# Fewer warm-up products, and four of the first pair's maxima between its first score groups

## The chip, the cores and the metric

One core of a Trainium2 chip runs the whole program. The metric is the time of one execution in microseconds on the device, as a median of runs; smaller is better. The engines are named as in the profile: PE is TensorE (matrix products), PEld its weight load, DVE VectorE, ACT ScalarE, POOL GpSimd, and SP issues the DMA transfers.

## The reference

Three stages, one after the other, all in fp32:

```
q_pool = q.reshape(B, H, S // 2, 2, D).mean(axis=3)
scores = scale * np.matmul(q_pool, k.transpose(0, 1, 3, 2))
scores = scores - np.max(scores, axis=-1, keepdims=True)
attn = np.exp(scores)
attn = attn / (np.sum(attn, axis=-1, keepdims=True) + 1e-09)
x = np.matmul(attn, v)                    # B 4, H 8, S 1152, D 64
h = x @ w_in                              # 2304 tokens, 512 to 2048
g = np.where(h > 0.0, h, np.exp(np.minimum(h, 0.0)) - 1.0)
y = g @ w_out                             # 2048 to 512
...                                       # soft mixture of 8 experts over y
```

## The kernel before

**Attention.** The 32 heads are taken in 16 pairs. For a pair, q is loaded and neighbours summed (`pool_q`, line 556), q and k are transposed by PE against an identity and split into a high and a low part (`prep_q`, lines 574 to 583; `prep_k`, lines 597 to 605, in two pieces of six and three blocks). The score groups (line 682, 36 for a pair) hold keys on the partitions, so the maximum over keys has to be known before the exponential. It is found ahead, from products of the high parts alone: a maximum unit (line 613, `max_unit`) makes 128 query rows (64 in the last tile) times 384 keys for both heads in PSUM, and DVE reduces it (line 622, `max_red`). The first pair has 15 such units of its own: nine for the first half of its queries and six for the second, of these six three with 128 rows and three with 64. When a half is complete, `max_end` reduces once more (DVE, line 662), lays the result out as a row with three products (PE, line 658), and ACT writes its negative (line 666); a score group of that half adds this row as its last two products. The exponential is ACT's (line 694), the running sum of exponentials POOL's or DVE's (line 703), and the product with v is line 689. For the later pairs most maxima ride along inside the score groups of the pair before.

**PSUM.** Score groups, maximum units and transposes share three double banks (psA0, psA1, psS2), taken in turn. A unit holds its bank until DVE has reduced it, a score group until ACT has taken its exponential.

**Warm-up.** The first work of PE is a row of 100 products of a constant with itself (`warm`, line 723), into psC1; nothing reads them. psC1 is then used by the second piece of k.

**Order.** Every operation has a planned time. A planner sorts them by these times and by a cost model of its own, and writes out one fixed order for each engine; on the chip each engine works its list in that order and waits for what an entry needs. The times of the first pair's six units for its second half stand in the table `MAX1`, as distances in groups of two score steps and an offset; those of `max_end` stand in `DE`.

**After attention** come an ELU network in 32 slots (lines 850 and 889) and the soft mixture of experts, whose weights are loaded into buffers as these come free (line 1214).

Of the kernel before, what the change touches and what calls it, by code (L numbers as in the profile page):

```python
# [26 lines left out]
def act(n, psum=False):  # L27
    return n * 0.0009 + (0.135 if psum else 0.165)
# [22 lines left out]
class Plan:  # L51
# [11 lines left out]
    def add(self, t, eng, dur, fn, r=(), w=(), size=0.0, mode="F", port=False, fixed=False):  # L63
        if isinstance(eng, str):
            eng, dur = (eng,), (dur,)
        cls = (self.tag or str(self.phase)) + "".join(x.rstrip("0123456789") for x in w[0][:2] if isinstance(x, str)) + (eng[0] if len(eng) == 1 else "*")
        self.ops.append([t, len(self.ops), eng, dur, fn, r, w, size * (0.75 if self.phase == 2 else 1.0), BIAS[3 if self.tag else self.phase], t + PRI.get(cls, 0.0), cls, mode, port, fixed])
# [194 lines left out]
N3 = 10  # L262
TM2 = [-14.582, 27.792, 22.6349, 17.3721]
TDT = [0.625, 1.728, 6.6355, 1.2]
WARM = [100]
OFF = {'wi': -10.8492, 'wo': 0.9719, 'h': -0.5713, 'o': -0.4908}
EP = 1.3
SLOT = 14.8061
# [2 lines left out]
DQ = [-10, 0.61]  # L271
DK = [[-9, 0.3], [-9, 0.3]]
UC = -14
MAX1 = [[-4, 0.9], [-3, 0.9], [-3, 1.3], [-2, 0.4], [0, 0.9], [0, 1.3]]
MAX2 = [[[-7, 0.4], [-6, -0.1], [-5, -0.1], [-4, -0.1]], [[-2, -0.1], [-1, -0.1]]]
DE = [[-2, 0.3], [2, 0.5]]
SUMD = [[1, 0.1], [1, 0.3]]
# [8 lines left out]
def attention_moe_softmoe(  # L286
# [99 lines left out]
    def v3(ap, a):  # L386
        return ap.rearrange("p (a b) -> p a b", a=a)
# [152 lines left out]
    def load_q(p, t):  # L540
        b, h0 = heads(p)
        for j in range(2):
            dma(t, QR[:QP, j].rearrange("p c r d -> p c (r d)"), q[b, h0 + j].rearrange("(c p r) d -> p c (r d)", p=QP, r=2),
                [], [("QR", 0, j)], 295e3)

    def load_k(p, t):
        b, h0 = heads(p)
        for j in range(2):
            dma(t, KR[:, :, j], k[b, h0 + j].rearrange("(p c) d -> p c d", c=NC), [], [("KR", 0, j)], 295e3)

    def load_v(p, t):
        b, h0 = heads(p)
        dma(t, VR[p % 2], v[b, h0 : h0 + 2].rearrange("h (p c) d -> p h c d", c=NC), [], [("VR", p % 2)], 590e3, 0.45)

    def pool_q(p, t):
        add(t, ("DVE", "Pool") if p else ("DVE",), (dve(768), pool(768))[: 1 + (p > 0)], lambda e="DVE": ENG[e].tensor_tensor(  # L556
            NQt[:QP].rearrange("p c j d -> p j c d"), QR[:QP, :, :, 0, :], QR[:QP, :, :, 1, :], ALU.add),
            r=[("QR", 0, 0), ("QR", 0, 1)], w=[("NQ", 0)], port=True)

    def T(p, d, x):  # L560
        return (NU * p + 2 * d) * STEP + x

    def TG(p, d, x):
        return (NU * p + GU * d) * STEP + x

    TC = 0.5 * GU * STEP

    def prep_q(p, t):
        i = p % 2
        tok = ("S", "pq", p)  # L570

        def tr():
            for c in range(QC):
                nc.tensor.transpose(got(psS, tok)[:, c // 3, c % 3 * QP : (c % 3 + 1) * QP],  # L574
                                    NQt[:QP, c].rearrange("p j d -> p (j d)"), ident[:QP, :QP])

        def ps():
            return got(psS, tok)[:, :, :NH]

        hi, lo = v3(qkb["qh", i], 2), v3(qkb["ql", i], 2)  # L580
        add(t, "PE", QC * 0.109, tr, r=[("NQ", 0)], w=[tok, ("qh", i), ("ql", i)], fixed=True)
        add(t + 0.01, "ACT", act(NQ, True), lambda: nc.scalar.copy(hi, ps()), r=[tok], w=[("qh", i)])
        add(t + 0.02, "DVE", dve(NQ), lambda: nc.vector.tensor_tensor(lo, ps(), r32(hi), ALU.subtract), r=[tok, ("qh", i)], w=[("ql", i)])

    def prep_k(p, g, t):
        i = p % 2
        lo_c, hi_c = KG[g]
        m = hi_c - lo_c
        nb = m // 3
        tok = ("S", "pk", p, g) if nb == 2 else ("C", 1)  # L590

        def bk(x):
            return got(psS, tok)[:, x] if nb == 2 else psC[1]

        def tr():
            for x in range(m):
                nc.tensor.transpose(bk(x // 3)[:, x % 3 * P : (x % 3 + 1) * P], KR[:, lo_c + x].rearrange("p j d -> p (j d)"), ident)  # L597

        def ps():
            return got(psS, tok)[:, :, : 3 * P] if nb == 2 else v3(psC[1][:, : 3 * P], 1)  # L600

        hi, lo = (v3(qkb[n, i][:, lo_c * P : hi_c * P], nb) for n in ("kh", "kl"))
        add(t, "PE", m * 0.109, tr, r=[("KR", 0, 0), ("KR", 0, 1)], w=[tok, ("kh", i, g), ("kl", i, g)], fixed=True)
        add(t + 0.01, "ACT", act(m * P, True), lambda: nc.scalar.copy(hi, ps()), r=[tok], w=[("kh", i, g)])
        add(t + 0.02, "DVE", dve(m * P), lambda: nc.vector.tensor_tensor(lo, ps(), r32(hi), ALU.subtract),
            r=[tok, ("kh", i, g)], w=[("kl", i, g)])
# [21 lines left out]
    def max_unit(p, a, g, t):  # L628
        tok = ("S", "max", p, a, g)
        add(t, "PE", 0.172, lambda: max_mm(got(psS, tok), p, a, g, 2, 0), r=max_deps(p, g, 2), w=[tok], mode="R", fixed=True)  # L630
        max_red(tok, p, a, g, 2, 0, t + 0.01)

    carry, own = {}, {}
    for p in range(NP):
        own[p] = []
        cells = {h: [(a, g) for a in ((0, 1, 2), (3, 4))[h] for g in range(0, NM, 2)] for h in range(2)}
        if p == 0:
            own[p] = [(a, g, *((-7 + x // 2, 0.2 * (x % 2)) if GU == 2 else (-5 + x // 3, 0.2 * (x % 3)))) for x, (a, g) in enumerate(cells[0])]
            own[p] += [(a, g, *MAX1[x]) for x, (a, g) in enumerate(cells[1])]
            continue  # L640
# [9 lines left out]
    def max_end(p, h, t):  # L650
        i = p % 2
        tiles = (0, 1, 2) if h == 0 else (2, 3, 4)

        def row():
            for a in tiles:
                o, n = QT[a]
                lo, hi = max(o, h * NH), min(o + n, (h + 1) * NH)
                nc.tensor.matmul(psC[h][:D, lo - h * NH : hi - h * NH], lhsT=MZ[:, a].rearrange("p j m -> p (j m)"), rhs=IDR[:, lo - o : hi - o],
                                 start=True, stop=True)

        a0, a1 = tiles[0] if h == 0 else 3, tiles[-1] + 1
        add(t - 0.5, "DVE", 0.2, lambda: nc.vector.reduce_max(MZ[:, a0:a1, :, 0], MX[i][:, a0:a1], axis=AX.X),
            r=[("MX", i, a, g) for a in range(a0, a1) for g in range(NM) if (p, a, g) in cells_of], w=[("MZ", 0, a) for a in range(a0, a1)])
        add(t, "PE", 0.15, row, r=[("MZ", 0, a) for a in tiles], w=[("C", h)], mode="C", fixed=True)
        for j in range(2):
            add(t + 0.01 + 0.01 * j, "ACT", act(NH, True), lambda j=j: nc.scalar.mul(
                v3(qkb["nm", i], 2)[j * D : j * D + D // 2, h], psC[h][j * D // 2 : (j + 1) * D // 2, :NH], -1.0), r=[("C", h)], w=[("nm", i, h, j)])
# [59 lines left out]
    def warm_first(n):  # L727
        f = MEM["v"][:, ND - 256 :]
        add(-101, "DVE", 0.5, lambda: None, w=[("vone", 0)])
        warm(n, -99.9, f, [("vone", 0)])  # L730
# [17 lines left out]
    for p in range(NP):  # L748
        if p == 0:
            plan.tag = "P"  # L750
            warm_first(WARM[0])
        load_q(p, T(p, -19.5, 0))
        load_k(p, T(p, -16.5, 0))
        load_v(p, T(p, -6, 0))
        pool_q(p, T(p, -11, 0))
        prep_q(p, TG(p, DQ[0], TC + DQ[1]))
        for g in range(2):
            prep_k(p, g, TG(p, DK[g][0] if p else (-9 if GU == 2 else -6), TC + DK[g][1] + 0.01 * g))
        for a, g, d, y in own[p]:
            max_unit(p, a, g, TG(p, d, y))  # L760
        for h in range(2):
            max_end(p, h, TG(p, DE[h][0], TC + DE[h][1]))
        plan.tag = None
        for u in range(NU):
            step(p, u)
# [608 lines left out]
```

## Time and profile before

| | |
|---|---|
| median of three runs | 1008.2 us (1007.24 to 1009.51) |
| the profiled execution | 1009.69 us, with a span of 1007.9 us |
| mean granted clock of PE | 0.981 |
| PE busy | 968.3 us, 96% |
| DVE busy | 763.3 us, 76% |
| ACT busy | 497.0 us, 49% |
| POOL busy | 396.8 us, 39% |

The profile is of one execution. Starts are in microseconds from the start of its span; a granted clock of 1.00 is full speed (2.4 GHz) and 0.50 is half (1.2 GHz). Matrix products are pipelined, so one that is shown as 280 ns long can be followed by the next after 118 ns; the distance of two starts says what one costs.

### The profile page before, as it was taken

Reading aid. Unit: us, or ns where it says so; the run is one execution under the profiler, and the core shown is the slowest. Engines: PE = TensorE matmul, PEld = TensorE weight load, DVE = VectorE, ACT = ScalarE, POOL = GpSimd, SP = SyncE. Lnnn points to the kernel's source line nnn. Section 1 sums busy time; section 2 is a strip of 40 time slices with the busy share of each in tenths; the row PEclk is TensorE's granted clock in tenths of the full one; section 3 lists DMA queues with packets and bytes.
Section 4 is the critical chain, followed back from the end, with each engine's and each line's share of the span. In section 5 each row is a group of like instructions: output and inputs, shape, how many; then the busy total and the mean of one; then the engine's idle time right before and its main releaser. Section 6 shows DMA issues by size and latency. Waiting matters only on the chain.

```text
span 1007.9 us, 21047 instructions
## 1 busy us (share of the span) xinstructions
PE 968.3 (96%) x8550; PEld 791.4 (79%) x8550; DVE 763.3 (76%) x1281; ACT 497.0 (49%) x887; POOL 396.8 (39%) x278
## 2 busy tenths in 40 slices
PE   7999999999999999999999999999999999998965
PEld 5677777766777767666899999999999999996422
DVE  4777788888878788899998899889857887765103
ACT  1466565565666656565664444434434475443102
POOL 1588879878888878887300000000000000000000
PEclk9799999999999999999999999999999999998997
DMA  7233323325334323221263233324430132315798
GB/s 170 47 78 79 82 64 103 90 61 157 97 84 103 84 67 82 62 68 34 78 224 106 99 114 107 116 84 152 152 123 26 42 123 88 119 49 230 258 379 281
DMA packets 101584, 114.88 MB, mean 114 GB/s; under 512 B 43632, under 2 KB 70768, under 8 KB 101488
## 3 DMA queue, kind: packets, MB, share of 16 engines
q1 hardware_dynamic: 101488, 113.55, 36.9%
q8 instruction: 67, 1.10, 0.4%
q14 instruction: 29, 0.24, 0.1%
HBM read 100.27 MB, written 13.18 MB: 113 GB/s over the span
## 4 chain that ended last, share of the span: by engine, by line
PE 83%; DVE 9%; DMA 5%; issue 1%; ACT 1%; SPq 1%; DVEq 0%; POOL 0%; ACTq 0%; POOLq 0%
PE psC L889 20%; PE psA L850 20%; PE psC L689 13%; PE psA L682 10%; PE psS L682 4%; DMA memf<-in_moe_w_dram 3%; PE psA L613 3%; DVE memf L622 2%; PE psS L613 2%; PE psC L723 1%; PE psC L713 1%; PE psA L597 1%; DMA memzq<-in_moe_w_dram 1%; DVE memf L556 1%; PE psA L574 1%
## 5 line engine op out<-in xcount | busy, mean ns | idle before, releaser
L703 POOL TENSOR_TENSOR memf<-memf 128x576 f32<-128x576 f32 x241 | 360.2, 1497 | 62.7 <-ACT memf L694 38.3
L889 PE MATMUL psC<-memr,memz 128*128 128x288 f32 x1512 | 224.7, 297 | 1.2 <-DVE memf L900 0.7
L889 PEld LDWEIGHTS psC<-memr,memz 128*128 128x128 f32 x1512 | 208.1, 188 | 4.4 <-ACT memf L508 1.6
L689 PE MATMUL psC<-memf 128*64 128x288 f32 x1152 | 174.2, 419 | 0.0
L694 ACT ACTIVATE memf<-psA 128x576 f32<-128x576 f32 x207 | 133.5, 652 | 63.7 <-PE psA L613 51.1
L622 DVE TENSOR_REDUCE memf<-psA 128x2 f32<-128x384 f32 (+3 forms) x236 | 143.3, 619 | 27.2 <-PE psA L613 13.0
L1334 POOL MEMSET memf<- 128x2048 f32 x1 | 1.8, 1811 | 388.5 <-DVE memr L511 388.5
L900 DVE TENSOR_TENSOR memf<-psC,memf 128x288 f32<-128x288 f32 x220 | 100.3, 463 | 47.9 <-PE psC L889 46.2
L622 DVE TENSOR_REDUCE memf<-psS 128x2 f32<-128x384 f32 (+1 forms) x139 | 102.6, 738 | 35.3 <-PE psS L613 18.7
L689 PEld LDWEIGHTS psC<-memf 128*64 128x64 f32 x1152 | 69.8, 136 | 48.5 <-issue 9.2
L850 PE MATMUL psA<-memz 128*128 128x288 f32 x512 | 93.8, 295 | 0.0
L861 ACT ACTIVATE memf<-psA 128x576 f32<-128x576 f32 x64 | 41.8, 654 | 103.1 <-PE psA L850 103.0
L508 ACT CAST memr<-memf 128x576 fp32r<-128x576 f32 x72 | 48.2, 675 | 74.3 <-PE psC L889 35.9
L850 PEld LDWEIGHTS psA<-memz 128*128 128x128 f32 x512 | 76.6, 188 | 0.0
L682 PE MATMUL psA<-memr 64*128 64x288 f32 x816 | 72.2, 299 | 2.9 <-DVE memf L622 2.9
L694 ACT ACTIVATE memf<-psS 128x576 f32<-128x576 f32 x81 | 52.8, 652 | 39.3 <-PE psS L613 35.9
L511 DVE TENSOR_TENSOR memr<-memf,memr 128x576 fp32r<-128x576 f32 x80 | 62.8, 791 | 6.5 <-ACT memr L508 6.0
L682 PEld LDWEIGHTS psA<-memr 64*128 64x128 f32 x816 | 59.2, 185 | 9.7 <-DVE memf L622 4.8
L682 PE MATMUL psA<-memy 64*128 64x288 f32 x630 | 62.6, 304 | 0.1
L850 PE MATMUL psA<-memz,memv 128*128 128x288 f32 x256 | 52.0, 296 | 0.0
L682 PEld LDWEIGHTS psA<-memy 64*128 64x128 f32 x630 | 47.8, 188 | 4.9 <-issue 3.6
L508 ACT COPY memf<-psC 128x288 f32<-128x288 f32 (+1 forms) x66 | 26.3, 398 | 49.5 <-PE psC L1265 26.6
(213 smaller groups left out, 1623.2 us busy)
## 6 DMA issues: line engine op xcount, KB each, us to landing
memf<-wscr SPq DMA_DIRECT2D x32, 512.0 KB
memf<-in_moe_w_dram SPq DMA_DIRECT2D x30, 512.0 KB
memzq<-in_moe_w_dram SPq DMA_DIRECT2D x22, 512.0 KB
memz<-in_q_dram SPq DMA_DIRECT2D x32, 288.0 KB
memz<-in_k_dram SPq DMA_DIRECT2D x32, 288.0 KB
memf<-in_v_dram SPq DMA_DIRECT2D x16, 576.0 KB
memf<-in_moe_w_in_dram SPq DMA_DIRECT2D x32, 256.0 KB
wscr<-memf SPq DMA_DIRECT2D x32, 256.0 KB
```

The costliest lines, as they stand in the source:

```text
L508: return lambda e: nc.scalar.copy(out_, in_) if e == "ACT" else nc.vector.tensor_copy(out_, in_)
L511: return lambda e: ENG[e].tensor_tensor(out_, a, b, ALU.subtract)
L613: nc.tensor.matmul(tile_[:m, j, lo : lo + n * MW], lhsT=qkb["qh", i][js, o : o + m], rhs=qkb["kh", i][js, g * MW : (g + n) * MW], start=Tr ...
L622: add(t, "DVE", dve(2 * n * MW), lambda: nc.vector.reduce_max(MX[i][:m, a, :, g : g + n], v4(got(psS, tok)[:m, :, lo : lo + n * MW], n), a ...
L682: nc.tensor.matmul(sp[:, j, :NH], lhsT=qkb[w, i][js, cs] if w else ONER[js], rhs=qkb[m, i][js, hs], start=(x == 0), stop=(x == 3))
L689: nc.tensor.matmul(psC[h][j * D : (j + 1) * D, :NH], lhsT=VR[i][:, j, c], rhs=e[:, j], start=(c == 0), stop=(c == NC - 1))
L694: add(t + 0.01, "ACT", act(NQ, True), lambda: nc.scalar.activation(got(EAf, E_), got(psS, S_)[:, :, :NH], AF.Exp, scale=1.0 / 16.0), r=[S_ ...
L703: ENG[e].tensor_tensor(ac, a, got(EAf, E_), ALU.add)
L850: nc.tensor.matmul(ph[:, t, :NH], lhsT=a, rhs=x, start=(i == 0), stop=(i == 3 * KD - 1))
L861: add(t, "ACT", act(NQ, True), lambda: nc.scalar.activation(got(Ef, uk), ph(), AF.Relu, scale=-1.0), r=[A], w=[uk])
L889: nc.tensor.matmul(po_(), lhsT=a, rhs=x, start=(i == 0), stop=(i == 3 * GF - 1))
L900: add(t0 + 0.8, "DVE", dve(NH), lambda: nc.vector.tensor_tensor(d, po_(), d, ALU.add), r=[ck], w=XK)
```

## The change

The warm-up has 24 products in place of 100. The table `MAX1` gives the six units of the second half other times, all later, and the first pair's `max_end` gets a table `DE1` of its own, whose times are 0.3 and 0.1 us later than in `DE`.

```
-WARM = [100]
+WARM = [24]
...
-MAX1 = [[-4, 0.9], [-3, 0.9], [-3, 1.3], [-2, 0.4], [0, 0.9], [0, 1.3]]
+MAX1 = [[-2, 0.4], [-2, 1.3], [0, -0.1], [0, 0.9], [1, -0.1], [1, 1.3]]
+DE1 = [[-2, 0.6], [2, 0.6]]
...
-            max_end(p, h, TG(p, DE[h][0], TC + DE[h][1]))
+            max_end(p, h, TG(p, (DE if p else DE1)[h][0], TC + (DE if p else DE1)[h][1]))
```

The lines of the changed kernel below the tables are one higher than before. On PE, the piece from the eleventh unit to just ahead of the third score group stands so before (`ident` with `memf` is the transpose of the second pair's q, `ident` with `memz0` that of its k, line 682 a score group in two rows):

```order
L613 MATMUL psA0_78<-memy_95 128x384 x2
L613 MATMUL psA1_79<-memy_95 128x384 x2
L613 MATMUL psS2_85<-memy_95 64x384 x2
L658 MATMUL psC0_80<-memv_94 64x128 x2
L658 MATMUL psC0_80<-memv_94 64x32
L574 MATMUL psA0_78<-ident_65,memf_93 128x96 x6
L682 MATMUL psA1_79<-memy_95 128x288 x6
...
L613 MATMUL psA1_79<-memy_95 64x384 x2
L613 MATMUL psA0_78<-memy_95 64x384 x2
L597 MATMUL psS2_85<-ident_65,memz0_96 128x128 x6
L597 MATMUL psC1_81<-ident_65,memz0_96 128x128 x3
```

And so in the changed kernel, up to the first product with v:

```order
L614 MATMUL psA0_78<-memy_95 128x384 x2
L659 MATMUL psC0_80<-memv_94 64x128 x2
L659 MATMUL psC0_80<-memv_94 64x32
L575 MATMUL psA1_79<-ident_65,memf_93 128x96 x6
L614 MATMUL psS2_85<-memy_95 128x384 x2
L683 MATMUL psA0_78<-memy_95 128x288 x6
...
L614 MATMUL psA0_78<-memy_95 64x384 x2
L598 MATMUL psA1_79<-ident_65,memz0_96 128x128 x6
L598 MATMUL psC1_81<-ident_65,memz0_96 128x128 x3
L614 MATMUL psS2_85<-memy_95 64x384 x2
...
L614 MATMUL psA0_78<-memy_95 64x384 x2
L690 MATMUL psC0_80<-memf_93 64x288 x4
```

The end of the first half's maxima (line 658, now 659) has moved ahead of two units. The twelfth unit now stands right ahead of the first score group, and the three units of 64 rows stand one behind the second score group, one behind the transposes of k and one behind the fourth score group. From the product with v on the order is the one of before, but for the numbers in the names.

On DVE, the same stretch before, from the tenth reduction on:

```order
L622 TENSOR_REDUCE memf<-psS_85 128x2x2
L662 TENSOR_REDUCE memv<-memf 128x6
L622 TENSOR_REDUCE memf<-psA_78 128x2x2
L622 TENSOR_REDUCE memf<-psA_79 128x2x2
L622 TENSOR_REDUCE memf<-psS_85 64x2x2
L1112 TENSOR_TENSOR memr<-phi_sb,memr 128x4x32
L583 TENSOR_TENSOR memr<-psA_78,memr 128x576
L622 TENSOR_REDUCE memf<-psA_79 64x2x2
L622 TENSOR_REDUCE memf<-psA_78 64x2x2
L662 TENSOR_REDUCE memv<-memf 128x4
L605 TENSOR_TENSOR memr<-psS_85,memr 128x768
L605 TENSOR_TENSOR memr<-psC_81,memr 128x384
```

And in the changed kernel:

```order
L663 TENSOR_REDUCE memv<-memf 128x6
L623 TENSOR_REDUCE memf<-psS_85 128x2x2
L623 TENSOR_REDUCE memf<-psA_78 128x2x2
L623 TENSOR_REDUCE memf<-psS_85 128x2x2
L584 TENSOR_TENSOR memr<-psA_79,memr 128x576
L1113 TENSOR_TENSOR memr<-phi_sb,memr 128x4x32
L623 TENSOR_REDUCE memf<-psA_78 64x2x2
L623 TENSOR_REDUCE memf<-psS_85 64x2x2
L606 TENSOR_TENSOR memr<-psA_79,memr 128x768
L606 TENSOR_TENSOR memr<-psC_81,memr 128x384
L623 TENSOR_REDUCE memf<-psA_78 64x2x2
L663 TENSOR_REDUCE memv<-memf 128x4
```

The small reduction that ends the first half (line 662, now 663) comes behind the ninth unit in place of the tenth, and the low part of the second pair's q (line 583, now 584) comes ahead of that of phi (line 1112, now 1113). On SP one thing moves: the two loads of the second pair's k now stand ahead of the two of phi. On ACT the second cast of the second pair's k moves ahead of two exponentials, and POOL's list is unchanged.

## Rows read from the trace of the kernel before

**Rows 1.** Page: busy time of each engine, share of the span, instructions.

```profile
PE 968.3 (96%) x8550; PEld 791.4 (79%) x8550; DVE 763.3 (76%) x1281; ACT 497.0 (49%) x887; POOL 396.8 (39%) x278
```

**Rows 2.** Busy time by stage: PE, PEld, DVE, ACT, POOL, clock, DMA share, GB/s.

```profile
38.00:100.00 62.00, 61.43 (x657) 44.16 (x655) 43.58 (x67) 37.27 (x66) 52.91 (x37) 1.00 0.31 73
...
940.00:1008.00 68.00, 46.88 (x435) 21.13 (x427) 10.79 (x33) 10.51 (x28) 0.00 (x0) 0.89 0.96 338
```

**Rows 3.** Chain that ended last, first 41 us: start, length, what.

```profile
3.06 13.62 PE psC L723 x100
...
20.12 8.65 DVE memf L622 x10
```

**Rows 4.** Timeline of PE, three windows: start, length from first to last, products.

```profile
3.06 1.49 PE L723 MATMUL psC<-memv 128*32 128x256 f32 x6 [3.06 <-DVE memv L516]
...
13.80 2.87 PE L723 MATMUL psC<-memv 128*32 128x256 f32 x23
16.52 0.66 PE L574 MATMUL psA<-ident,memf 96*128 96x96 f32 x6
17.01 0.82 PE L597 MATMUL psA<-ident,memz 128*128 128x128 f32 x6
```

**Rows 5.** Timeline of the first 20 us: the sum of q, and SP's issue of the second pair's k.

```profile
5.26 0.95 DVE L556 TENSOR_TENSOR memf<-memz 96x768 f32<-96x768 f32 x1 [1.83 <-DMA memz<-in_q_dram]
...
18.19 1.32 SPq L514 DMA_DIRECT2D memz<-in_k_dram  x2
```

**Rows 6.** Busy time by stretch of the first 8 us; the last column is GB/s.

```profile
0.00:5.20 5.20, 2.14 (x11) 1.71 (x12) 2.10 (x5) 1.49 (x2) 2.61 (x14) 1.00 0.69 163
5.20:6.70 1.50, 1.50 (x9) 1.19 (x8) 0.95 (x1) 0.00 (x0) 0.00 (x0) 1.00 1.38 231
```

**Rows 7.** Busy time by stretch from the maxima on; PE first, the clock third from the end.

```profile
19.00:23.80 4.80, 2.27 (x14) 0.96 (x12) 4.80 (x7) 0.25 (x2) 0.09 (x1) 1.00 0.94 206
23.80:30.00 6.20, 4.81 (x18) 2.05 (x18) 6.17 (x9) 0.07 (x1) 0.00 (x0) 0.50 0.16 30
30.00:33.80 3.80, 3.80 (x24) 3.02 (x24) 3.80 (x4) 2.37 (x5) 1.83 (x1) 0.50 0.00 0
33.80:37.50 3.70, 3.48 (x19) 2.81 (x19) 2.66 (x5) 1.10 (x2) 1.41 (x1) 0.50 0.64 159
37.50:41.00 3.50, 3.50 (x42) 2.59 (x40) 1.38 (x3) 2.22 (x4) 2.27 (x2) 1.00 0.78 173
```

**Rows 8.** Timeline of DVE, 27 to 34 us.

```profile
27.82 0.94 DVE L622 TENSOR_REDUCE memf<-psS 128x4 f32<-128x768 f32 x1
28.80 0.19 DVE L662 TENSOR_REDUCE memv<-memf 128x6 fp32r<-128x36 f32 x1
...
33.23 0.74 DVE L583 TENSOR_TENSOR memr<-psA,memr 128x576 fp32r<-128x576 f32 x1
```

**Rows 9.** Timeline of PE, from the end of the first maxima to the fifth score group.

```profile
29.33 0.50 PE L658 MATMUL psC<-memv 128*64 128x128 f32 x3
30.00 1.19 PE L574 MATMUL psA<-ident,memf 96*128 96x96 f32 x6 [0.17 <-DVE memf L622]
31.12 1.09 PE L682 MATMUL psA<-memy 64*128 64x288 f32 x6
...
34.03 0.58 PE L613 MATMUL psA<-memy 64*64 64x384 f32 x2 [0.22 <-DVE memr L583]
34.54 1.54 PE L597 MATMUL psS<-ident,memz 128*128 128x128 f32 x6
...
36.65 1.04 PE L682 MATMUL psA<-memy 64*128 64x288 f32 x6
...
38.28 1.19 PE L689 MATMUL psC<-memf 128*64 128x288 f32 x8
39.40 0.66 PE L682 MATMUL psA<-memy 64*128 64x288 f32 x6
...
40.03 0.25 PE L613 MATMUL psA<-memr 64*128 64x192 f32 x2
```

## The prediction

> **What bounds the kernel now.** I began with the busy times: PE is at work for 96% of the span [rows 1]. That is an average, so I took it by stage: from 38 to 100 us PE is busy for 61.43 of 62 us at full clock, while DVE, ACT and POOL have 19, 25 and 9 us to spare [rows 2]. In that stretch a microsecond saved ahead of it is saved at the end. Only the last stage has another limit: from 940 us on PE is busy for 47 of 68 us and the DMA engines for 96%, at 338 GB/s [rows 2]. Its loads go into buffers that earlier work leaves, so it moves with that work.
>
> The change lies in the first 40 us, so I then followed the chain that ended last through these. It runs through all 100 warm-up products, 13.62 us from 3.06 on, and later through 8.65 us of reductions on DVE [rows 3]. So up to 16.5 us PE's row of products that nobody reads sets the end; from 20 to 29 us DVE does, one unit every 0.865 us (8.65 over ten); from 30 us on it is PE again. There its clock matters: it is at full speed to 23.8 us, at half from 23.8 to 37.5, and full afterwards [rows 7].
>
> **Term 1: 76 warm-up products less.** The first six take 1.49 us to the end of the last. With 0.42 us of that as the length of one at half speed (twice 0.21), their distance is (1.49 - 0.42) / 5 = 0.214 us. The last 23 take 2.87 us: (2.87 - 0.28) / 22 = 0.118 us [rows 4]. From 3.06 to 16.40, the start of the last, are 99 steps, which gives 17 or 18 at 0.214 us and a change at 6.8 us. So 24 products hold all of those and six or seven at 0.118 us, and what goes are 76 of the latter: 76 x 0.118 = **8.95 us**. They end at about 7.5 us, and the transposes of q begin at 16.52 - 8.95 = 7.57 in place of 16.52 [rows 4].
>
> What was hidden behind the 100 products must now be ready. The sum of q ends at 5.26 + 0.95 = 6.21 [rows 5]. The first k is issued behind q, and both are 1.18 MB (four transfers of 288 KB). By 5.2 us 163 GB/s x 5.2 = 0.85 MB had moved, and 231 GB/s bring the rest by 6.7 us [rows 6]. The q's 0.59 MB were so moved near 4.2 us, and their reader began at 5.26, 1.1 us later; k should so be there at about 7.8. Its transposes come 0.49 us behind those of q [rows 4], at 8.06. That is an estimate with a margin of 0.3 us; were k a microsecond late, a microsecond is lost.
>
> On SP the second k's loads now stand ahead of phi's. They wait for the first k's buffer (issued at 18.19 before [rows 5], so at 9.24), and phi queues behind their 0.59 MB, some 2.6 us at 231 GB/s. ACT casts phi ahead of the negative maxima, which it can take from about 19.5 us on. I expect phi at about 17 us and price this at nothing; its bound is the delay beyond 19.5.
>
> The reductions stay DVE's at 0.865 us each at either clock: the PE row is 2.27 of 4.80 us at full speed and 4.81 of 6.20 at half, with DVE full in both [rows 7]. Should PE fall to half speed already among the transposes, these cost some 0.5 to 0.9 us more (six at half speed take 1.19 us, at full speed 0.66 [rows 9, 4]); I take none.
>
> **A rule beside it.** The Trainium skill, "TensorE: Matmul & The Clock Gate", Part 1, says that what releases the clock is a time of activity and not a number of products, and that the moment isn't tied to the kernel's start. In this trace it came after 3.7 us of products, so 24 were enough by 0.8 us. By the rule another execution can reach the end of 24 products, 5.1 us at half speed, without release. It would be the mechanism of the first rival.
>
> **Term 2: the order of the units.** I keep the old time scale for this, without term 1. The small reduction of line 662 now follows the ninth unit in place of the tenth: it starts 0.87 us earlier than 28.80, and line 658 about 0.9 earlier than 29.33, at 28.4 [rows 8, 9]. Then come the transposes of the second q (1.12 us, 30.00 to 31.12) and the twelfth unit (0.51, as from 34.03 to 34.54) [rows 9]; with 0.6 for the three row products the first score group starts at about 30.67 in place of 31.12, so 0.45 earlier. Before, from it to the first product with v (38.28) PE took 7.16 us [rows 9]. It now has one unit of 64 rows more there. All at half speed that is four groups of 1.05, three units of 0.51 and the nine transposes, 36.65 - 34.54 = 2.11: 7.84 us. All at full speed it is four of 0.63 (39.40 to 40.03 [rows 9]), and half of the rest: 4.4 us.
>
> Which clock? Before, it came back at the end of a stretch from 34.03 to 37.5 in which PE never stopped; ahead of it PE had stood for 0.22 us at 34.03, for DVE [rows 7, 9]. In the new order I find no such stop from 28.9 on: each bank is free when its turn comes, since one unit, and not two, stands between groups. So I choose a return inside this stretch, neither at its first group nor behind it, at 34: then 3.3 us run at half speed and the other 4.54 in 2.6, 5.9 us. DVE sets a floor: between the twelfth unit and the fourth group stand three unit reductions, line 583 (0.74 [rows 8]) and phi's small one, about 3.7 us, and a group, a wait for its exponential and a unit follow, 5.0 us in all. So close to that floor I add 0.7 us of waiting: 6.6. Term 2 is 0.45 + 7.16 - 6.6 = **1.0 us** gained. Its ends are 0.45 + 7.16 - 7.84 = -0.2 (half speed throughout) and 0.45 + 7.16 - 5.0 = +2.6.
>
> **Sum.** 8.95 + 1.0 = 9.95 us. The profiled execution has a span of 1007.9 and took 1009.69, so its sum is 997.95 and 999.7. It is 1.5 us above the median of 1008.2, which gives **998.3** as the median after.
>
> **The rivals.**
> - *The clock comes back late.* The maxima keep PE at half load, and 24 products leave it no reserve; half speed lasts over the transposes (+0.7), through all of term 2 (-0.2 in place of 1.0) and 3 us into the stage behind, where half speed costs half of it, 1.5. Gain 8.95 - 0.7 - 0.2 - 1.5 = 6.55: 1001.7, and 1002.7 with a microsecond of spread. For it speaks that 3.8 us of full PE from 30.0 to 33.8 didn't bring the clock back before [rows 7]. Against it, that the new order has no stop there. The Trainium skill, "TensorE: Matmul & The Clock Gate", "A second HAM failure mode: psum-queue depth-cycling", says that short idles between groups of products that cycle through PSUM make the clock swing.
> - *A load is late.* k a microsecond behind its turn, or phi in front of the negative maxima: 1 to 2 us of the gain, 999.8.
> - *The gain is given back* by a bound that doesn't start with PE, POOL in attention or the weight loads at the end: 1008. Against it: POOL has 9 of 62 us free [rows 2], and the loads follow freed buffers.
> - *Slower.* PE stays at half speed in the first pair's steady steps, since the maxima of DVE stop it once in each. Half speed costs half of its length, so it eats 9.95 us in 20 us and is 0.2% (2 us) slower from 24 us on, up to about 53 us of the new scale, 1010.5. Against it: at half speed PE is the slowest engine, so it has no stops, and before full speed came back at the first such stretch [rows 7].
>
> **Chances.** My forecast 0.60, the late clock 0.22, a late load 0.11, given back 0.04, slower 0.03. Runs before spread over 2.3 us, about 0.2%, and 0.2% is about what a measurement of this kernel can tell from no change: faster 0.93, same 0.04, slower 0.03. The range goes from the best of both terms with a microsecond of spread (1008.2 - 8.95 - 2.6 - 1.0 = 995.7) to the late clock, 1002.7.
>
> **What would show it.** Warm-up: 24 products from 3.06 to about 7.5 us, transposes right behind, first reduction near 11.1. If transposes start later, k was late or the clock was not released. Term 2: line 659 at about 19.5, the first score group near 21.7, the first product with v near 28.3 us (38.28 - 9.95), and full clock back between 23.5 and 27. If that product comes at 29.5 or later, term 2 is wrong. If it is right and the end is not 10 us earlier, the loss is later, and the stages must show where.

## The result, and the profile after

The changed kernel takes 997.83 us as a median of six runs (995.99 to 1000.3), the kernel before 1008.85 us in the same rounds (six runs, 1007.24 to 1011.05). The ratio is 0.9898 with a 95% interval of 0.988 to 0.9915: about 1.0% faster. The forecast was 998.3 us in a range of 995.7 to 1002.7. The profiled execution took 997.68 us with a span of 995.6 us.

The timeline of PE, from its first product to the first product with v (start, length, operation, in brackets PE's idle time ahead and who ended it), which answers to [rows 4, 9]:

```profile
2.38 4.88 PE L724 MATMUL psC<-memv 128*32 128x256 f32 x24 [2.38 <-DVE memv L517]
7.10 0.66 PE L575 MATMUL psA<-ident,memf 96*128 96x96 f32 x6
7.99 0.85 PE L598 MATMUL psA<-ident,memz 128*128 128x128 f32 x6 [0.23 <-DMA memz<-in_k_dram]
...
19.18 0.50 PE L659 MATMUL psC<-memv 128*64 128x128 f32 x3 [0.41 <-DVE memv L663]
...
21.16 0.92 PE L683 MATMUL psA<-memy 64*128 64x288 f32 x6
...
26.49 0.81 PE L683 MATMUL psA<-memy 64*128 64x288 f32 x6
...
27.81 0.67 PE L683 MATMUL psS<-memy 64*128 64x288 f32 x6 [0.37 <-DVE memf L623]
...
28.71 1.19 PE L690 MATMUL psC<-memf 128*64 128x288 f32 x8
29.83 0.67 PE L683 MATMUL psA<-memy 64*128 64x288 f32 x6
```

The transposes of q began at 7.10 in place of 16.52 and were not held up. Those of k came 0.89 us behind them, where they had come 0.49 behind in [rows 4]: their load landed only at 7.85 us. That is 0.40 us lost, of which the profile lists 0.23 as idle time of PE. The first product with v began 38.28 - 28.71 = 9.57 us earlier than in [rows 9].

DVE and ACT in the same stretch, from their timelines, beside [rows 8]:

```profile
11.04 0.95 DVE L623 TENSOR_REDUCE memf<-psS 128x4 f32<-128x768 f32 x1
...
18.93 0.19 DVE L663 TENSOR_REDUCE memv<-memf 128x6 fp32r<-128x36 f32 x1
...
17.30 0.30 ACT L509 CAST memr<-phi_sb 128x128 fp32r<-128x128 f32 x1 [7.25 <-DMA phi_sb<-in_moe_phi_dram]
19.79 0.82 ACT L667 ACTIVATE memy<-psC 32x288 fp32r<-32x288 f32 x2 [2.19 <-PE psC L659]
```

The reductions start at 11.04 (20.04 before [rows 3]). ACT did stand for 7.25 us in front of the cast of phi, whose load now comes last, and was through 2.19 us before the negative maxima needed it.

The chain that ended last, first 22 us: start, length, what.

```profile
2.43 5.42 DMA memz<-in_k_dram
...
7.99 0.86 PE psA L598 x6
...
11.12 7.79 DVE memf L623 x9
```

Where the 100 products stood in [rows 3], the chain now runs through k's load.

Busy time by stretch, beside [rows 7] (PE first, the granted clock third from the end):

```profile
6.50:13.30 6.80, 4.33 (x31) 2.88 (x29) 4.44 (x7) 1.82 (x3) 0.00 (x0) 1.00 1.14 290
13.30:19.00 5.70, 4.17 (x14) 1.73 (x12) 5.67 (x8) 0.30 (x1) 1.81 (x1) 0.51 0.86 152
19.00:27.00 8.00, 7.72 (x46) 6.35 (x48) 4.82 (x8) 3.92 (x7) 3.22 (x2) 0.50 0.44 113
27.00:31.00 4.00, 3.63 (x40) 2.50 (x40) 3.13 (x5) 1.54 (x3) 2.65 (x2) 0.99 0.72 152
```

PE's clock fell to half at 13.4, among the units, and came back at 27.0. The first two score groups, the second k's transposes and half of the third group lie in the half-clock stretch.

### The profile page after: what moved, and what is told of

It is laid out like the page before. It is cut to its first block, busy times and chain, and to the rows that moved or that the text cites. A ratio compares the mean times of both kernels' runs of the same rounds, so it can differ in the third digit from the quotient of the medians.

```text
span 995.6 us, 20896 instructions
## 1 busy us (share of the span) xinstructions
PE 958.6 (96%) x8474; PEld 783.5 (79%) x8474; DVE 760.4 (76%) x1281; ACT 496.9 (50%) x887; POOL 396.3 (40%) x278
## 4 chain that ended last, share of the span: by engine, by line
PE 85%; DVE 8%; DMA 4%; ACT 1%; SPq 1%; issue 1%; DVEq 0%; ACTq 0%
PE psC L890 20%; PE psA L851 20%; PE psC L690 14%; PE psA L683 10%; PE psS L683 5%; PE psA L614 3%; PE psS L614 3%; DVE memf L623 2%; DMA memf<-in_moe_w_dram 2%; PE psC L714 1%; PE psA L598 1%; PE psA L1230 1%; DMA memzq<-in_moe_w_dram 1%; PE psA L575 1%; DVE memf L557 1%; PE psC L659 1%
## 5 line engine op out<-in xcount | busy, mean ns | idle before, releaser
L623 DVE TENSOR_REDUCE memf<-psS 128x4 f32<-128x768 f32 (+1 forms) x140 | 103.5, 740 | 38.3 <-PE psS L614 20.5
```

Of the source, the lines that this page charges most:

```text
L623: add(t, "DVE", dve(2 * n * MW), lambda: nc.vector.reduce_max(MX[i][:m, a, :, g : g + n], v4(got(psS, tok)[:m, :, lo : lo + n * MW], n), a ...
```

## The experiments

All runs are of the whole kernel, with the kernel before in the same rounds. To read the short stretches apart from the rest I use two marks of each profile: the start of the first unit's reduction, and that of the first product with v.

**Each half alone.** The kernel before with fewer products:

```
-WARM = [100]
+WARM = [24]
```

> The kernel before with 24 warm-up products in place of 100 and nothing else. Theory (the products are the gain): the first reduction of a unit begins 8.3 to 9 us earlier than at 20.04, the first product with v 8.3 to 9.3 us earlier than at 38.28, and the time is about 9 us below that of before, ratio 0.990 to 0.992. Rival (the new order makes a third or more of the gain): no more than 7 us, ratio 0.993 or above.

Measured: ratio 0.9899 (0.9884 to 0.9914), as much as the whole change. The marks and the transposes of k, from the timelines:

```profile
8.13 0.85 PE L597 MATMUL psA<-ident,memz 128*128 128x128 f32 x6
...
11.19 0.95 DVE L622 TENSOR_REDUCE memf<-psS 128x4 f32<-128x768 f32 x1
...
28.87 1.19 PE L689 MATMUL psC<-memf 128*64 128x288 f32 x8
```

The first reduction is 8.85 us earlier than before and the product with v 9.41, a little more than expected. The rival is out.

The changed kernel with the 100 products back:

```
-WARM = [24]
+WARM = [100]
```

> The changed order of the units with all 100 warm-up products. Theory (order is worth 0.6 us, as the change's trace has it between the first reduction and the first product with v): that product 0.3 to 1.2 us earlier than at 38.28, time within 0.2% of before, ratio 0.998 to 1.000. Rival (order is worth 2 us or more, the measured 11 us less the 9 of the products): ratio 0.998 or below. A second rival (order costs, since PE has a unit more in the half-clock stretch): product later than 38.3.

Measured: ratio 0.9998 (0.9987 to 1.0009). The marks:

```profile
18.59 0.95 DVE L623 TENSOR_REDUCE memf<-psS 128x4 f32<-128x768 f32 x1
...
35.55 1.19 PE L690 MATMUL psC<-memf 128*64 128x288 f32 x8
```

The product with v is 2.73 us earlier than before, but 1.45 of that stands ahead of the first reduction, where the order plays no part. The marks lie 35.55 - 18.59 = 16.96 us apart, against 38.28 - 20.04 = 18.24 before, 1.28 us better, a little above the theory's upper end. But this execution had half clock for about 10 us, 22.3 to 32.4, against 13.7 us in [rows 7], so the clock is part of that. In the pair with 24 products, where full clock returns at 27.3 and 27.0 us, the marks are 17.68 us apart with the old order and 17.67 with the new. In time the order alone is worth nothing that can be measured, and by the marks nothing in the pair whose clock returned alike.

**How far the warm-up is still on the path.** The changed kernel with `WARM = [8]`:

> The changed kernel with 8 warm-up products in place of 24. Theory (the first k's load is now what PE waits for, as its 0.23 us ahead of the transposes of k says): the transposes of k stay at 7.7 to 8.1 us, the first reduction moves by less than 0.7 us from 11.04, and the time is within 0.15% of the changed kernel. Rival (the warm-up still sets the end): 16 products of 0.21 us less, 3.4 us earlier, 0.34% below the changed kernel. Second rival (without a warm-up of 5 us full clock comes back later in the score groups): 1.7 us or more above the changed kernel.

Measured: ratio 0.9902 (0.9885 to 0.9918), within 0.15% of the change. Transposes of k at 8.07, first reduction at 11.79. PE's timeline:

```profile
3.05 1.91 PE L724 MATMUL psC<-memv 128*32 128x256 f32 x8 [3.05 <-DVE memv L517]
6.50 1.19 PE L575 MATMUL psA<-ident,memf 96*128 96x96 f32 x6 [1.54 <-DVE memf L557]
8.07 1.51 PE L598 MATMUL psA<-ident,memz 128*128 128x128 f32 x6 [0.37 <-DMA memz<-in_k_dram]
```

The reader sees PE wait twice, for the sum of q and for k. What 16 products less would have given is waited away, and the transposes, at half clock, take 1.19 and 1.51 us in place of 0.66 and 0.85; the first reduction was 0.75 us later, a little more than I had allowed. The second rival is out too: full clock came back at 25.1 us, earlier than the change's 27.0, and the first product with v stood at 28.45, ahead of the change's 28.71.

With `WARM = [0]`:

> The changed kernel without any warm-up product. Theory (k's load sets the start; the transposes run at half clock and cost some 0.7 us more, as with 8 products): transposes of k at 7.7 to 8.1 us, first reduction at 11.5 to 11.9, time within 0.2% of the changed kernel. Rival (the warm-up buys an earlier return of full clock in the score groups): full clock back 3 us or more later than with 24, and 1.5 us or more slower.

Measured: ratio 0.9913 (0.9891 to 0.9936), 0.15% above the change and within the intervals of both. Transposes of k at 7.83, first reduction at 11.55, product with v at 29.23. By the lengths of its products PE ran at half speed up to 27.5 us, so full clock did not come 3 us later than with 24, and by this mark the rival fails; its 1.5 us in time could not have been told from nothing here. By the product with v, 24 products are 0.5 us ahead of none and 0.3 us behind 8. No run shows that the warm-up as a whole is worth anything.

With `WARM = [62]`:

> The changed kernel with 62 warm-up products, half of the 76 put back. Theory (each is 0.118 us on the path once k is there): the transposes of k begin 38 x 0.118 = 4.5 us later than with 24, less the 0.4 us for which PE waits for k there, so at 11.9 to 12.7 us, and the time is 0.35 to 0.5% above the changed kernel. Rival (the gain is a step, because the products beyond some number collide with the loads): no change or the whole 9 us.

Measured: ratio 0.9943 (0.9923 to 0.9964), 0.45% above the change. PE's timeline:

```profile
2.39 8.65 PE L724 MATMUL psC<-memv 128*32 128x256 f32 x62 [2.39 <-DVE memv L517]
10.88 0.66 PE L575 MATMUL psA<-ident,memf 96*128 96x96 f32 x6
11.38 0.82 PE L598 MATMUL psA<-ident,memz 128*128 128x128 f32 x6
...
31.85 1.19 PE L690 MATMUL psC<-memf 128*64 128x288 f32 x8
```

The transposes of k come 3.4 us later than in the change, half a microsecond less than the least expected. Those of q come 3.78 us later and not 4.48, since the clock was released at 5.5 us here and at 6.6 in the change, so that fewer products ran at half speed; 0.40 of the 3.78 is the change's wait for k. The product with v is 3.14 us later. The gain is no step: half of the products put back take back about half of it.

**What half clock costs.** The changed kernel with further products of the constant in the waits between the units:

```
+FILL = [2, 11, 3]
...
+            if p == 0 and FILL[0] <= x < FILL[1]:
+                fill(FILL[2], TG(p, d, y) + 0.005)
```

`fill(n, t)` adds n products as the warm-up's, into psC1.

> The changed kernel with three further products of the constant behind each of nine maximum units, where PE otherwise waits for DVE (27 in all, at most 0.35 us of them in a wait of 0.42 us at full clock). Theory (half clock in the first score groups costs what PE-bound work there takes twice): PE keeps full clock from 6.6 us on, the reductions stay 0.865 us apart, and the first product with v comes 2 to 3 us earlier than at 28.71, time 0.2 to 0.3% below the changed kernel. Rival (DVE's reductions and the waits for exponentials set the pace of those groups): full clock, but less than 1 us. Second rival (the products delay the units): reductions further apart than 0.9 us, later.

Measured: ratio 0.9897 (0.9881 to 0.9913), no better than the change. The marks are 27.26 - 11.96 = 15.30 us apart, against 17.67: the expected 2.4 us are there, at full clock throughout. But in this execution PE began at 3.05 us and the clock was released only at 8.7, so the transposes of k came at 8.93 and the first reduction 0.92 us late.

With 20 warm-up products and the same fill:

> The changed order with 20 warm-up products and three more products of the constant behind each of nine units, so that full clock lasts. Theory (at full clock the stretch from the first reduction to the first product with v takes 15.3 us, as in the earlier run with them, against 17.7 in the changed kernel): 15.2 to 15.5 us, and with the transposes of k at 7.7 to 8.2 us the product with v at 26 to 27 us, time 0.15 to 0.35% below the changed kernel. Rival (the gain of 2.4 us was that execution's): 16.5 us or more.

Measured: ratio 0.9900 (0.9881 to 0.992). Marks 15.30 us apart, k's transposes at 8.02, product with v at 26.37, all as the theory had it; the time is not: the ratio is no lower than the change's 0.9898.

The same with the order of before, 11 groups:

> The same with the order of the units of before (11 groups of three such products, since two more units stand ahead of the small reduction). It tells what the order is worth where the clock plays no part. Theory (the order is worth one reduction of 0.87 us, less a unit more of PE's work, as long as the clock is the same): the stretch from the first reduction to the first product with v takes 0.4 to 0.9 us longer than with the new order. Rival (the order is worth 2 us without the clock's fall): 1.5 us or more longer. Second rival (the order is worth nothing): within 0.2 us.

Measured: ratio 0.9932 (0.9905 to 0.9959), 0.34% above the change, though the intervals overlap, with runs from 997.37 to 1005.29. The question was not answered, since here the clock fell at 12.4 us all the same. PE's timeline then:

```profile
14.57 0.69 PE L615 MATMUL psA<-memy 64*128 64x384 f32 x2
15.19 0.85 PE L732 MATMUL psC<-memv 128*32 128x256 f32 x3
15.97 0.69 PE L615 MATMUL psS<-memy 64*128 64x384 f32 x2
```

A unit with its three products takes 15.97 - 14.57 = 1.40 us in place of 0.865: PE, not DVE, sets the pace, and the added work delays the units. In these kernels the added products began only behind the third unit.

So the next three begin them behind the first unit and put them into psC0, which has no reader until the maxima end, with 24 warm-up products. Three each:

```
+FILL = [0, 11, 3]
...
+                psC[0][:NS, :256], lhsT=f[:, :NS], rhs=f, start=True, stop=True),
```

> The changed kernel with three more products of the constant behind each of the first eleven units, now into psC0, which nothing else uses until the first maxima end, so that they wait for no reader. Theory (PE then never falls to half clock ahead of the first product with v): full clock from the warm-up on, 15.2 to 15.5 us from the first reduction to that product, time 0.15 to 0.35% below the changed kernel. Rival (the clock falls between the transposes and the third unit, and at half clock three products make a unit 1.1 us or more in place of 0.865): half clock in the stretch, 17 us or more.

The same with the order of before (`FILL = [0, 13, 3]`):

> The same with the order of the units of before and 13 groups of three. At full clock in both the difference is that of the order alone. Theory (one reduction of 0.865 us less ahead of the first score group, one unit more of PE's work behind it): from the first reduction to the first product with v 0.4 to 0.9 us more than with the new order. Rival (two units less ahead of it, 1.7 us): 1.5 us or more. Second rival: within 0.2 us.

Two each with the new order (`FILL = [0, 11, 2]`):

> The changed kernel with two such products behind each of the first eleven units. At half clock they would lengthen a unit less than three do. Theory (two are enough to keep full clock): as with three, 15.2 to 15.5 us from the first reduction to the first product with v. Rival (two are too few): half clock for 3 us or more within the stretch, 16 us or more, no better than the changed kernel.

And the changed kernel itself beside them:

> The changed kernel itself, on the chip and in the rounds of the three kernels with more products, so that they can be compared. All theories: ratio to before 0.988 to 0.992, full clock back between 24 and 28 us, 17 to 18 us from the first reduction to the first product with v.

| kernel | ratio to before | median, us | range, us | first reduction | first product with v | apart |
|---|---|---|---|---|---|---|
| three products, new order | 0.9884 (0.9868 to 0.99) | 997.22 | 995.98 to 997.38 | 11.65 | 26.95 | 15.30 |
| three products, old order | 0.9894 (0.9877 to 0.9911) | 997.17 | 996.48 to 999.08 | 11.29 | 27.48 | 16.19 |
| two products, new order | 0.9882 (0.9865 to 0.9898) | 996.88 | 995.61 to 997.47 | 11.42 | 26.71 | 15.29 |
| the change | 0.9914 (0.9898 to 0.9929) | 999.83 | 998.35 to 1001.25 | 11.03 | 28.68 | 17.65 |

Busy time by stretch with two products:

```profile
12.00:19.00 7.00, 6.42 (x34) 2.64 (x34) 7.00 (x9) 0.30 (x1) 1.81 (x1) 1.00 0.97 180
19.00:27.00 8.00, 6.61 (x62) 4.66 (x62) 7.21 (x11) 4.93 (x9) 4.19 (x3) 1.00 0.52 112
```

And the change in the same rounds:

```profile
12.00:19.00 7.00, 5.26 (x16) 2.21 (x16) 6.97 (x9) 0.30 (x1) 1.80 (x1) 0.56 1.02 194
19.00:27.00 8.00, 7.73 (x48) 6.33 (x48) 4.84 (x8) 3.92 (x7) 3.22 (x2) 0.53 0.32 81
```

DVE is full ahead of 19 us in both, so the products cost the units nothing at full clock. Behind it PE does 62 products where it did 48, in less busy time. The first reduction comes 0.3 to 0.6 us later in these executions, where the clock was released later in the warm-up (its 24 products took 4.88 to 5.33 us, those of the change 4.31), and 2.4 us are won behind it. All runs of both kernels with the new order are below all runs of the change in these rounds; their medians are 2.6 and 2.95 us lower. Two products, enough to keep full clock here, beat both kernels in these rounds; two and three can't be told apart. By the product with v the gain over the change is 1.7 and 2.0 us, so that not all of the 2.6 and 2.95 is shown to come from the clock in this stretch. Against the first set of the change (median 997.83, 0.9898) neither stands clear.

At full clock in both, the old order needs 16.19 us between the marks and the new one 15.30: the order is then worth 0.89 us, the theory's upper end, and one reduction. In time it is not seen, with medians of 997.17 and 997.22. Where the old order loses it is read from PE's timelines, first the old order's:

```profile
22.03 0.67 PE L684 MATMUL psA<-memy 64*128 64x288 f32 x6
...
23.60 0.39 PE L615 MATMUL psA<-memy 64*64 64x384 f32 x2
24.78 0.39 PE L615 MATMUL psA<-memy 64*64 64x384 f32 x2 [0.79 <-DVE memr L585]
...
27.48 1.19 PE L691 MATMUL psC<-memf 128*64 128x288 f32 x8
```

The new order's:

```profile
21.52 0.67 PE L684 MATMUL psA<-memy 64*128 64x288 f32 x6 [0.42 <-DVE memf L624]
...
26.05 0.67 PE L684 MATMUL psS<-memy 64*128 64x288 f32 x6 [0.59 <-DVE memf L624]
...
26.95 1.19 PE L691 MATMUL psC<-memf 128*64 128x288 f32 x8
```

From the first reduction to the first score group the old order takes 22.03 - 11.29 = 10.74 us and the new one 21.52 - 11.65 = 9.87, which is the reduction saved. From there to the product with v they take 5.45 and 5.43: behind the first group the order gains nothing. Each has its stop there. In the old order two units stand side by side, and the second waits 0.79 us for the bank whose reader, on DVE, is late (the stop of [rows 9], 0.22 us there at half clock). In the new one the fourth group waits 0.59 us until DVE has reduced the unit that held its bank.

## Why the prediction held, and where its terms were off

**The warm-up as the bound.** Right. The fewer products alone give the whole of the change's measured gain, 62 give a part, and 8 or none give no more than 24.

**Term 1, 8.95 us.** The first reduction of the change is 9.00 us earlier, with fewer products alone 8.85. This agreement hides three parts, which add up to the 9.0 (8.95 + 0.68 - 0.2 - 0.4). PE began 0.68 us earlier, at 2.38 in place of 3.06, which the kernel with 100 products and the new order shows too (2.39) and the one with 8 does not (3.05): it goes with the execution. Four or five products of the 24 ran at full clock, not six or seven, which cost 0.2. And k's load held the transposes by 0.40 us where I had a margin of 0.3, since PE came early. In the kernel with fewer products alone PE began at 2.91 us, and the load, whose last part landed at 8.00 by the trace, still held the transposes of k by 0.15 (8.13 - 7.49 less 0.49). So in both profiles it is k's landing, and no longer the warm-up, that sets their start. That the term came out to 0.1 us is in part luck, since these two limits lay that close together.

**What was hidden.** The estimates of k (there at about 7.8) and phi (17) were near: k's transposes were let go at 7.99, phi's cast began at 17.30 with 2.2 us to spare. The clock's fall among the units cost the units nothing, as I had it: the reductions still followed each other in 7.79 us for nine, 0.866 each.

**Term 2, 1.0 us, was too large.** Its first step is right, and was priced too low: the small reduction of line 663 came at 18.93, 0.87 us closer to the first reduction than before, and the first score group 0.96 closer, where I had 0.45. The step that failed is the stretch behind it, where I took the 7.16 us from the first group to the product with v down to 6.6 by an early return of the clock. I put that in the middle of the stretch, at 34 on the old scale, which is 25 us on the new one; it came at 27.0, with the third of the four score groups half done, and PE took 28.71 - 21.16 = 7.55 us. So of 0.96 us 0.4 went back, and the term is 18.24 - 17.67 = 0.57 us in the two profiles. In the pair whose clock returned alike (27.3 and 27.0) all of it went back: 6.59 us behind the first group with the old order, 7.55 with the new. In the pair with 100 products it is 1.28. In time it could not be seen, not even at full clock, where the marks say 0.89.

Two premises of that step did not hold. I had found no stop of PE in the new order, and there is one, 0.37 us ahead of the fourth group, which waits for the reduction of the unit that held its bank. In the second profile of the change it decides: full clock was back half a microsecond earlier, at 26.5, and the product with v came no earlier, since the stop grew:

```profile
27.78 0.66 PE L683 MATMUL psS<-memy 64*128 64x288 f32 x6 [0.58 <-DVE memf L623]
...
28.68 1.19 PE L690 MATMUL psC<-memf 128*64 128x288 f32 x8
```

The 0.7 us of waiting that I had added cover this stop. And the order does not fix the return: in the six profiles of the new order without added products full clock came back 13.3 to 16.0 us after the first reduction, and the marks lie 16.66 to 17.68 us apart. What decides the return was not tried.

**The rivals.** The late clock did not come to pass beyond that: full clock was back before the steady steps in every profile of a kernel without added products. Its mechanism, 24 products that end before the release, was seen in two kernels with added products. The clock was released at 8.7 us in the first one and at 8.3 in the one with two in each wait, behind the last of the 24 in both, and the first reduction came 0.92 and 0.38 us later than in the change. The late load of k did come to pass, with 0.40 us. Nothing was given back.

**The rest of the gain.** In the profiles the first product with v is 9.57 us earlier and the span 12.3 us shorter. The further 2.7 us come in places that the change does not touch. One is a wait of DVE for a small transfer. Before:

```profile
353.59 0.54 DVE L738 RECIPROCAL memf<-memf 18x64 f32<-18x64 f32 x1 [1.49 <-DMA memf<-memf]
```

After, at the same place:

```profile
343.40 0.54 DVE L739 RECIPROCAL memf<-memf 18x64 f32<-18x64 f32 x1 [0.47 <-DMA memf<-memf]
```

Another is the clock in the last stage, where the experts' first products begin. Before, by stretch:

```profile
935.00:941.00 6.00, 6.00 (x45) 1.64 (x47) 0.00 (x0) 0.39 (x2) 0.00 (x0) 0.72 0.28 84
```

After:

```profile
924.00:929.00 5.00, 5.00 (x48) 1.47 (x51) 0.00 (x0) 0.32 (x2) 0.00 (x0) 1.00 0.43 139
```

No run shows these to be the change's. Its second set of runs has its first product with v at 28.68, as the first, and a median 2.0 us higher: 999.83 us against 1008.85 before, a gain of 9.0 us, so that nothing is left there for other places. The forecast of 998.3 lies between the two medians of the change, 997.83 and 999.83. That it came within 0.5 us of the first is luck in part: it counted 1.0 us for term 2, which the time doesn't show, and left out what these places gave.

## What to carry to other kernels

Count a warm-up's products against the landing of the first load. Here those that ran on behind it were paid for as they ran (62 and 100 products), and those ahead of it were worth nothing that the time shows (0, 8 and 24). Where a stage ahead of PE-bound work is paced by another engine, PE's clock can fall in it. Here two or three products of a constant in each wait kept it when they began early; where it had fallen, three of them made a unit 1.40 us in place of 0.865. Compare two orders of such a stretch at one clock: by the marks this one was worth 0.9 us at full clock and nothing where the clock fell and returned alike, and a stop that it removed came back in another place.

## What the runs showed of the hardware

The stretch from the units to the first score groups ran at half clock for 10.2 to 13.7 us in each profile without added products, whether 100, 62, 24 or 8 products stood ahead; with none, PE was at half speed up to 27.5 us. The clock column of the profile does not show the beginning: it reads 1.00 there in every run, also in the first kernel with added products from 3 to 7 us, where 24 products took 8.17 - 3.05 = 5.12 us, 0.213 each. Releases ahead of the first fall are read from the distances and lengths of products. The Trainium skill, "TensorE: Matmul & The Clock Gate", Part 1, says that the moment of release is not tied to the kernel's start. The runs agree: products that began at 3.05 us were released at 6.0 us in the second profile of the change and at 8.7 us in the first kernel with added products. PE's start was 2.4 or about 3 us; it follows the first small copy on DVE, which takes 0.68 us in some executions and 1.2 to 1.35 in others:

```profile
1.33 0.68 DVE L335 COPY sel<-ident 128x16 f32<-128x16 f32 x1 [1.33 <-POOL ident masks.py:199]
```

That is the change; with 8 products it took 1.34 us. What decides it was not tried.
